# Order of the relu sums in the last token group, and of a product and a transpose early on

## The chip, the cores and the metric

The kernel runs on one core of a Trainium2 chip. The metric is device time in microseconds (us). Its time before the change is 225.6 us, the median of three runs (225.09, 225.60 and 230.58).

## What is computed

Attention with a window ("LM-infinite"), then a mixer. There are 4 batches (B), 8 heads (H) of width 64 (D) and 768 positions (S). Each query sees 8 global keys and the 96 keys up to itself:

```python
scores = scale * np.matmul(q, k.transpose(0, 1, 3, 2))
...
keep = is_global | is_local
...
scores = scores + bias          # -slope of the head * distance
scores = np.where(keep, scores, -1000000000.0)
a = np.exp(scores - max); a = a / sum(a)
attn = np.matmul(a, v)
```

The heads are put side by side to x of 768 x 512 per batch, and then

```python
h = xt @ U @ V                  # low rank, 32, over the positions
u = x + h.transpose(0, 2, 1)
ch = np.maximum(u @ w_ch1, 0.0) @ w_ch2      # 512 -> 2048 -> 512
return u + ch
```

Inputs and output are 32-bit floats; the kernel casts to 16 bits for its matmuls.

## The kernel before, in words

**Engines and order.** The program's order is written by hand: one `manual_schedule` covers it all, and each engine runs its own instructions in the order in which the code issues them. PE does matmuls and transposes, DVE and ACT the work between them and PE's accumulation banks, POOL casts, SP starts most loads and all stores. An instruction waits on the engine of its operands' producers, and on those who still use the buffer that it writes. Behind a waiting instruction its whole engine waits. PE's weight loads (PEld) run ahead of its matmuls.

**Pairs of heads.** The unit of the attention is a pair of heads: 4 pairs (NP) per batch, 16 in all, numbered through, so pairs 0 to 3 are batch 0 and pair 4 is the first of batch 1. In the main loop of batch 0 (L965 to L1011, one turn per pair i) these stages are issued:

- `st_T(i)` (L247): PE transposes q and k of a pair (twelve matmuls, L259). ACT copies qT (L281), DVE copies kT (L282) and a small part of kA (L287), the keys as the neighbouring block needs them, with the global ones in front.
- `st_KA(i)` (L292): DVE copies the rest of kA from kT (L295).
- `st_A(i)`, `st_P(i)` (L320): vA, the values as kA needs them. POOL copies it, and st_P has DVE put the 8 global rows in (L322).
- `st_SE(i, c)` (L381), a third c of the scores: matmuls with the bias on PE (L364, L372, L379), the exponential on ACT (L391, L396).
- `st_V(i, hi)` (L440), v's product for one head: eleven matmuls into a bank "ob" (L449, L453), DVE takes the reciprocals of the sums (L458), and DVE multiplies into x_sb (L472). In the last pair of batch 0 (pair 3) ACT multiplies head 0 straight into the 16-bit x (six instructions, L467), and DVE head 1 (L464); both write x16 of the same pair, in different columns. For head 1 of pairs 0 to 2, ACT copies x into the 16-bit x16 later (L1009, `last_x`).
- `st_M1(i)` (L478) multiplies x16 with U on PE (L492), DVE copies the result (L496). `st_M2(i)` (L504) multiplies with V and adds x (L509, L514); the result uT is copied by DVE (L520) or ACT (L522).
- `st_R()` (L400): DVE halves the bias table once (L402, "the table's half"), in turn 3.

For pair 3 (i = 3) the turn issues, in this order: scores, third 0; cast_v, st_A; st_V(2, 0); load_v(4); st_M1(1); scores, third 1; st_T(4); st_V(2, 1); st_KA(4); st_P(3); st_R; scores, third 2; the ACT copy L1009; st_M2(1). Behind the loop (L1012 on) follow st_V(3, 0), the first scores of pair 4, st_M1(2), st_V(3, 1), a cast on POOL (L124), st_M2(2), the first matmuls of the up-projection (L557), st_M1(3) and st_M2(3). From L1027 on comes the steady loop, in which the attention of later pairs is interleaved with the mixer's matmuls.

**The mixer.** The tokens of a batch form 3 groups of 256 (FT). Up-projection and relu give htr (16 blocks of 128 channels, L822 and L827; in batch 3 through seven products on sums, `queue_products`, L695 on PE, with L670 on DVE and L704, L745 on ACT). The down-projection of batches 1 to 3 goes by Winograd's variant of Strassen (`queue_group`, L781): htr is cut into a11, a12, a21, a22 (channel half by token half), and DVE forms

```
s1 = a21 + a22    s2 = s1 - a11    s3 = a11 - a21    s4 = a12 - s2
```

(`queue_sums`, L791, instruction L576; s3 overwrites a21). Each product (`mk_product`, L880) is eight matmuls on PE (L890) into one half of a bank, cx or cy, and then an add of that half into x_sb on DVE (L895). The products are x1 (a11), y1 (a12), x2 (s2), y2 (s1), x3 (s3), y3 (s4) and x4 (a22). In the last group of all (batch 3, group 2) they are issued x1, y2, x2, y1, x3, y3, and then `end_product` (L866), which takes the seventh in two halves of 128 columns (L872, L877) with a store behind each (L836).

A sum isn't issued to DVE when it is queued. `queue_sum` (L573) puts it into a list (`jobs` for the s, `slow` for the t, the sums of weights); `fill` (L930) takes it out when it is due, between two products. `need` (L580) takes sums out ahead of a product until the named ones are there. `queue_sums(k)` is called twice for each group: k = 0 when the first half of the channels' blocks is there, k = 1 with the second. s1 and s2 are made in two halves, one in each call. s3 and s4 are made whole in the second call, but in the last group in two halves too (128 x 512 each, in place of 128 x 1024). In the last group the second call comes right behind the last product of the up-projection (row (2, 1, 4): group 2, channel set 1, product 4), which is issued behind x1 and ahead of y2.

Of the kernel before, what the change touches and what calls it, by code (L numbers as in the profile page):

```python
# [20 lines left out]
def kernel(  # L21
# [24 lines left out]
    NP = H // 2  # L46
# [41 lines left out]
    def ps_cps(name, dtype=FP32, cols=512):  # L88
        return psum.tile([P, cols], dtype, name=name, tag="cps", bufs=2)

    def ps_th(name, dtype=FP32, cols=512):
        return psum.tile([P, cols], dtype, name=name, tag="th", bufs=3)
# [74 lines left out]
    def warm(n, cols=512):  # L167
        wps = ps_cps("warm")
        for _ in range(n):
            nc.tensor.matmul(wps[:, 0:cols], zw[:, 0:P], zw[:, 0:cols], start=True, stop=True)  # L170
# [76 lines left out]
    def st_T(i):  # L247
        stq, stk = cast.pop(i)
        qT = kp.tile([P, S], FP16, name="qT", tag="qT")
        kT = kp.tile([P, S], FP16, name="kT", tag="kT")  # L250
        kA = kp.tile([P, NSB - 1, P], FP16, name="kA", tag="kA")
        tps = []
        for st in (stq, stk):
            if i == 0 and st is stk:
                warm(4, P)
            tp = ps_th("tp", FP16, S) if i < NP + 2 else ps_cps("tp", FP16, S)
            tps.append(tp.rearrange("d (n p) -> d p n", n=NSB))
            for n in range(NSB):
                nc.tensor.matmul(  # L259
                    tp[:, n * P:(n + 1) * P], st[:, n].rearrange("s h d -> s (h d)"), ident16,  # L260
                    is_transpose=True, start=(n == 0), stop=(n == NSB - 1),
                )
        tq, tk = tps
        qts[i] = qT
        if i == 0:
            kts[i], kas[i] = kT, kA
            for a in range(2):
                ts, ps = slice(a * GT, (a + 1) * GT), slice(a * P // 2, (a + 1) * P // 2)
                nc.scalar.copy(qT[:, ts].rearrange("d (p n) -> d p n", n=NSB), tq[:, ps])
                nc.vector.tensor_copy(kT[:, ts].rearrange("d (p n) -> d p n", n=NSB), tk[:, ps])  # L270
                ns = slice(0, 2) if a == 0 else slice(2, NSB - 1)
                nc.vector.tensor_copy(
                    kA[:, ns].rearrange("d n p -> d (n p)"), kT[:, ns.start * P:ns.stop * P]
                )
                ns = slice(max(1, ns.start), ns.stop)
                nc.vector.tensor_copy(
                    kA[:, ns, 0:NG],
                    kT[:, 0:NG].unsqueeze(1).broadcast_to((P, ns.stop - ns.start, NG)),
                )
            return  # L280
        nc.scalar.copy(qT.rearrange("d (p n) -> d p n", n=NSB), tq)  # L281
        nc.vector.tensor_copy(kT.rearrange("d (p n) -> d p n", n=NSB), tk)  # L282
        kts[i], kas[i] = kT, kA
        if i > NP:
            st_KA(i, nc.gpsimd)
        else:
            nc.vector.tensor_copy(  # L287
                kA[:, :, 0:GC].rearrange("d b (p n) -> d b p n", n=NSB),
                tk[:, 0:GC // NSB].unsqueeze(1).broadcast_to((P, NSB - 1, GC // NSB, NSB)),
            )  # L290

    def st_KA(i, eng):  # L292
        kT, kA = kts[i], kas[i]
        if i <= NP:
            eng.tensor_copy(  # L295
                kA[:, :, GC:], kT.rearrange("d (n p) -> d n p", n=NSB)[:, 0:NSB - 1, GC:]
            )
            return
        eng.tensor_copy(kA.rearrange("d n p -> d (n p)"), kT[:, 0:S - P])
        eng.tensor_copy(  # L300
            kA[:, 1:, 0:NG], kT[:, 0:NG].unsqueeze(1).broadcast_to((P, NSB - 2, NG))
        )
# [17 lines left out]
    def st_P(i):  # L320
        eng = nc.gpsimd if i == NPE - 1 else nc.vector
        eng.tensor_copy(  # L322
            vas[i][0:NG, 1:].rearrange("p n h d -> p n (h d)"),
            vts[i][0:NG, 0:1].rearrange("p n h d -> p n (h d)").broadcast_to(
                (NG, NSB - 2, 2 * (D + 1))
            ),
        )
# [72 lines left out]
    def st_R():  # L400

        nc.vector.tensor_scalar_mul(relcat2[:, 1], relcat, 0.5)  # L402
# [170 lines left out]
    def queue_sum(name, part, out_, a, b_, op, wait=0):  # L573

        def go():
            nc.vector.tensor_tensor(out_, a, b_, op)  # L576
            have.add((name, part))
        (slow if name[0] == "t" else jobs).append((count[0] + wait, go, name))

    def need(*names):  # L580

        for queue, kind in ((jobs, tuple), (slow, str)):
            while not all(n in have for n in names if isinstance(n[0], kind)):
                queue.popleft()[1]()
# [19 lines left out]
    def weight(w, j):  # L604
        return tw[w][:, j] if w != "t3" else tw[w][j // 2][:, j % 2]
# [175 lines left out]
    def queue_group(b, g):  # L781
# [7 lines left out]
        last = (b, g) == (B - 1, NFG - 1)  # L789

        def queue_sums(k):  # L791

            h = cell["htr"]
            if k == 0:
                for x in (1, 2, 4):
                    cell[f"s{x}"] = ffp.tile([P, HJ, P], FP16, name=f"s{x}", tag=f"s{x}", bufs=1)
                cell.update(a11=h[:, 0:HJ, 0:P], a12=h[:, HJ:NJC, 0:P],
                            a21=h[:, 0:HJ, P:FT], s3=h[:, 0:HJ, P:FT], a22=h[:, HJ:NJC, P:FT])
            for name, a, b_, op in (
                ("s1", "a21", "a22", ALU.add), ("s2", "s1", "a11", ALU.subtract),  # L800
                ("s3", "a11", "a21", ALU.subtract), ("s4", "a12", "s2", ALU.subtract),
            ):
                parts = {k: slice(k * HJ // 2, (k + 1) * HJ // 2)}
                if name in ("s3", "s4") and not last:
                    parts = {0: slice(0, HJ)} if k else {}
                for part, js in parts.items():
                    queue_sum(
                        (name, b, g), part, cell[name][:, js], cell[a][:, js], cell[b_][:, js],
                        op, wait=0 if last else 2 - k,
                    )  # L810
# [69 lines left out]
        def mk_product(bank, half, a, w, dst, first=False, done=None, more=()):  # L880

            def go():
                if bank not in cell:
                    cell[bank] = ps_cps(bank)
                need(*(((a, b, g), k) for k in range(2 if last or a in ("s1", "s2") else 1)
                       if a[0] == "s"))
                need(*((w, k) for k in range(4 if w == "t3" else 2) if w[0] == "t"))
                ps = cell[bank][:, half]
                for j in range(HJ):
                    nc.tensor.matmul(  # L890
                        ps, cell[a][:, j], weight(w, j), start=(first and j == 0),
                        stop=(done is not None and j == HJ - 1), skip_group_check=True,
                    )
                for n, cs in (dst, *more):
                    nc.vector.tensor_tensor(x_sb[:, n, cs], ps, x_sb[:, n, cs], ALU.add)  # L895
                for what in done or ():
                    store(*what)
            return go
# [66 lines left out]
    for i in range(NP):  # L965
        st_SE(i, 0)
        cast_v(i)
        st_A(i)
        if i:
            st_V(i - 1, 0)  # L970
        if i == 0:
            load_uv()
        if i < 2:
            load_v(i + 2)
        if i == 1:
            load_qk(NP)
        if i == 2:
            load_qk(NP + 1, nc.gpsimd)
        if i == 3:
            load_v(NP)  # L980
        if i == NP - 1:
            st_M1(i - 2)
        if 0 < i < NP - 1:
            st_T(i + 1)
        st_SE(i, 1)
        if i == NP - 1:
            st_T(i + 1)
        if i == 2:
            st_M1(i - 2)
        if i:  # L990
            last_x = st_V(i - 1, 1)
        else:
            st_T(i + 1)
        st_KA(i + 1, nc.vector)
        st_P(i)
        if i == 0:
            cast_qk(i + 2, nc.vector)
        elif i < 3:
            cast_qk(i + 2, nc.gpsimd)
        if i == 1:  # L1000
            nc.gpsimd.tensor_copy(u16[:, :, 0:R], ust)
            load_w1(0)
        if i == 2:
            load_w1(1)
        if i == NP - 1:
            st_R()
        st_SE(i, 2)
        if i:
            nc.scalar.copy(*last_x)  # L1009
        if i >= 2:  # L1010
            st_M2(i - 2)  # L1011
# [15 lines left out]
    for i in range(NP, NPAIR + 2):  # L1027
        b, hp = divmod(i, NP)
# [140 lines left out]
```

## Time and profile before

| what | value |
|---|---|
| runs, all (us) | 225.09, 225.60, 230.58 |
| their median (us) | 225.60 |
| the profiled execution, its own time (us) | 224.96 |
| its span, first to last instruction (us) | 223.2 |
| PE's granted clock over the span | 1.00 |

The span is 1.76 us shorter than the execution's own time. Times in rows of the trace count from the span's start. In a row of the timeline stand the start, the length, the engine, the line, the operation and its tiles with sizes, and in brackets how long the engine was idle ahead of it and who ended that wait. In the chain of waits, which is followed back from the last instruction, "issue" is time in which the engine waited for nothing that the profile shows. Instructions of one engine overlap in the rows where the next one's start lies ahead of the last one's end.

### The profile page before, as it was taken

What the parts mean: (1) busy time and instruction counts of PE and PEld (TensorE: products, weight loads), DVE (VectorE), ACT (ScalarE), POOL (GpSimd) and SP (SyncE); (2) the same over time, 40 slices, a digit from 0 to 9 for tenths busy, and PEclk for the clock granted to TensorE, in tenths of its full rate; (3) what the DMA queues carried; (4) which work ended last, traced back from release to release, by engine and by line L of the source; (5) the groups of instructions that cost most, each with busy time, mean ns of one, the idle gap of its engine ahead of it and who ended that gap; (6) DMA issues with size and microseconds to landing.
All of it is one profiled execution on the core that took longest, in us unless ns stands there. A gap on an engine that the chain in (4) does not pass through costs nothing.

```text
span 223.2 us, 6285 instructions
## 1 busy us (share of the span) xinstructions
PE 216.3 (97%) x2577; PEld 172.5 (77%) x2579; DVE 174.8 (78%) x360; ACT 135.7 (61%) x215; POOL 74.0 (33%) x124
## 2 busy tenths in 40 slices
PE   7989999999999999999999999999999999999994
PEld 3556678788754546888888888888989999999973
DVE  3698775749488988598979698979798588878774
ACT  6787967785806253968594847382833556556620
POOL 6499638297547422322222222323112000000000
PEclk9999999999999999999999999999999999999999
DMA  6999999979998989898999995855240601102022
GB/s 200 327 290 245 261 229 260 319 142 173 195 171 177 200 212 258 207 255 190 212 249 205 241 222 118 156 147 38 80 82 17 117 0 50 50 3 94 3 94 95
DMA packets 86709, 36.75 MB, mean 165 GB/s; under 512 B 74169, under 2 KB 83737, under 8 KB 86681
## 3 DMA queue, kind: packets, MB, share of 16 engines
q1 hardware_dynamic: 82408, 32.11, 62.5%
q0 software_dynamic: 4272, 4.24, 12.4%
q8 instruction: 20, 0.33, 0.6%
q14 instruction: 9, 0.07, 0.1%
HBM read 27.46 MB, written 6.29 MB: 151 GB/s over the span
## 4 chain that ended last, share of the span: by engine, by line
PE 90%; DVE 7%; ACT 2%; issue 1%
PE hps L822 27%; PE cx L890 13%; PE cy L890 10%; PE cps L857 10%; PE hps L695 6%; PE sc L372 4%; PE tp L259 3%; PE ob L453 3%; PE ob L449 2%; PE sc L538 2%; PE warm L170 2%; PE sc L379 2%; PE ob L695 1%; PE sc L695 1%; PE sc L364 1%; DVE x_sb L895 1%
## 5 line engine op out<-in xcount | busy, mean ns | idle before, releaser
L822 PE MATMUL hps<-uT,w 128*128 128x256 f16 x564 | 70.6, 273 | 0.0
L827 ACT ACTIVATE htr<-hps 128x512 f16<-128x512 f32 x72 | 42.2, 601 | 33.4 <-PE hps L822 33.3
L822 PEld LDWEIGHTS <-w 128*128 128x128 f16 x564 | 52.4, 98 | 6.8
L418 DVE SCALAR_TENSOR_TENSOR sp<-sc,relcat 128x1024 f32<-128x1024 f32 (+1 forms) x27 | 32.1, 1188 | 8.3 <-PE sc L379 4.1
L436 ACT ACTIVATE ep<-sp 128x1408 f16<-128x1408 f32 x24 | 33.2, 1384 | 0.0
L475 POOL CAST x<-x_sb 128x384 f16<-128x384 f32 x27 | 14.2, 526 | 48.5 <-DVE x_sb L472 45.3
L890 PEld LDWEIGHTS <-htr 128*128 128x128 f16 x280 | 25.9, 98 | 2.8
L857 PE MATMUL cps<-w,htr 128*128 128x512 f16 x96 | 23.9, 379 | 0.0
L890 PEld LDWEIGHTS <-s 128*128 128x128 f16 x216 | 19.8, 98 | 3.4 <-DVE s L576 1.0
L546 POOL CAST x<-x_sb 128x768 f16<-128x768 f32 x12 | 10.6, 884 | 33.3 <-DVE x_sb L543 29.9
L895 DVE TENSOR_TENSOR x_sb<-cx,x_sb 128x256 f32<-128x256 f32 x36 | 15.0, 418 | 8.3 <-PE cx L890 7.9
L372 PEld LDWEIGHTS <-kT 64*128 64x128 f16 x192 | 8.7, 93 | 11.5 <-issue 10.1
L472 DVE TENSOR_TENSOR x_sb<-ob,rcp 128x384 f32<-128x384 f32 x30 | 16.7, 557 | 1.1
L745 ACT ACTIVATE htr<-htr 128x512 f16<-128x512 f16 x18 | 11.3, 630 | 9.3 <-DVE htr L670 9.3
L453 PE MATMUL ob<-v,ep 128*128 128x65 f16 x192 | 16.3, 194 | 0.3 <-DVE x_sb L472 0.3
L372 PE MATMUL sc<-qT,kT 64*128 64x128 f16 x192 | 15.7, 220 | 0.3
L453 PEld LDWEIGHTS <-ep 128*128 128x128 f16 x192 | 13.7, 98 | 2.7 <-issue 0.5
L895 DVE TENSOR_TENSOR x_sb<-cy,x_sb 128x256 f32<-128x256 f32 x27 | 11.3, 420 | 5.3 <-PE cy L890 4.9
L857 PEld LDWEIGHTS <-htr 128*128 128x128 f16 x96 | 8.4, 97 | 8.3
L449 PE MATMUL ob<-vA,ep 128*128 128x65 f16 x160 | 14.3, 194 | 0.3 <-DVE vA L322 0.2
L143 POOL CAST v<-vst 128x768 f16<-128x768 f32 x16 | 13.5, 842 | 3.2 <-DMA vst<-in_v_dram 3.2
L543 DVE TENSOR_TENSOR x_sb<-sc,x_sb 128x768 f32<-128x768 f32 x12 | 11.5, 958 | 3.7 <-PE sc L538 3.6
(141 smaller groups left out, 419.2 us busy)
## 6 DMA issues: line engine op xcount, KB each, us to landing
qst<-in_q_dram SPq DMA_DIRECT2D x16, 384.0 KB, 3.8
kst<-in_k_dram SPq DMA_DIRECT2D x16, 384.0 KB, 6.3
vst<-in_v_dram SPq DMA_DIRECT2D x16, 384.0 KB, 4.7
out_dram<-x_sb SPq DMA_DIRECT2D x23, 256.0 KB, 2.1
w<-in_moe_w_ch_dram POOLq DMA_DIRECT2D x8, 512.0 KB, 8.6
vA<-v SPq DMA_DIRECT2D x8, 152.3 KB, 3.4
uT<-x SPq DMA_TRANSPOSE x12, 4.5
kT<-k SPq DMA_TRANSPOSE x8, 3.2
```

What stands on the lines that cost most here:

```text
L372: nc.tensor.matmul(scs[hi][:, o:o + P], kT[r, kb * P:(kb + 1) * P], qT[r, kb * P:(kb + 1) * P], start=(o == 0 and not on_pe), stop=(o + P ...
L418: nc.vector.scalar_tensor_tensor(out=sps[i][:, :, c0:c0 + tot], in0=both[:, :, 0:tot], scalar=qk_scale / slope[2 * (i % NP)], in1=relfs[c0 ...
L436: nc.scalar.activation(eps[i][:, hi], sps[i][:, hi], AF.Exp, scale=slope[2 * (i % NP)])
L449: nc.tensor.matmul(ob[:, qi], ep[:, OF[qi - 1]:OF[qi - 1] + P], vA[:, qi - 1, hi], start=True, stop=False,)
L453: nc.tensor.matmul(ob[:, qi], ep[:, DG[qi]:DG[qi] + P], vt[:, qi, hi], start=(qi == 0), stop=True,)
L472: nc.vector.tensor_tensor(xo, ob[:, :, 0:D], rb, ALU.mult)
L695: nc.tensor.matmul(ps[:, j * P:(j + 1) * P], uw[st][a][:, dc, j * P:(j + 1) * P], turns[g][t][:, dc], start=(k in (1, 2, 5) and j == 0 and ...
L822: nc.tensor.matmul(hps[:, k * FT:(k + 1) * FT], w1_16[:, dc, jt * P:(jt + 1) * P], uT[:, dc, ts], start=(dc == 0 and k == 0), stop=(dc == ...
L827: nc.scalar.activation(cell["htr"][:, 2 * jp:2 * jp + 2].rearrange("p j t -> p (j t)"), hps, AF.Relu)
L857: nc.tensor.matmul(cps, htr[:, jc, t * P:(t + 1) * P], w2_16[:, jc], start=(b > 0 and jc == 0), stop=(jc == NJC - 1),)
L890: nc.tensor.matmul(ps, cell[a][:, j], weight(w, j), start=(first and j == 0), stop=(done is not None and j == HJ - 1), skip_group_check=True,)
L895: nc.vector.tensor_tensor(x_sb[:, n, cs], ps, x_sb[:, n, cs], ALU.add)
```

## The change

There are two parts, with no instruction added to PE and no DMA touched.

Part 1, the last group of the mixer. s3 and s4 are formed whole, in the second call of `queue_sums`, as in the other groups; so two instructions replace four. `mk_product` no longer asks for two halves of s3 and s4 there. Ahead of y2 (the product with s1) it asks for the second half of s2, and then for both halves of s1; as the jobs stand in one list, s1's second half, then s2's second half are issued ahead of y2. s3 is then issued when it is due or when x3 asks for it, s4 likewise with y3, behind s1 and s2.

Part 2, turn i = 3 of the loop of batch 0. `st_V(2, 1)` is issued ahead of `st_T(4)`, where it came behind it; `st_P(3)` is issued ahead of `st_KA(4)`, where it came behind it. The other turns issue what they did, in the same order.

```diff
@@ queue_sums
                 parts = {k: slice(k * HJ // 2, (k + 1) * HJ // 2)}
-                if name in ("s3", "s4") and not last:
+                if name in ("s3", "s4"):
                     parts = {0: slice(0, HJ)} if k else {}
@@ mk_product
                     cell[bank] = ps_cps(bank)
-                need(*(((a, b, g), k) for k in range(2 if last or a in ("s1", "s2") else 1)
+                if last and a == "s1":
+                    need((("s2", b, g), 1))
+                need(*(((a, b, g), k) for k in range(2 if a in ("s1", "s2") else 1)
                        if a[0] == "s"))
@@ main loop of batch 0
         st_SE(i, 1)
-        if i == NP - 1:
-            st_T(i + 1)
         if i == 2:
             st_M1(i - 2)
         if i:
             last_x = st_V(i - 1, 1)
-        else:
+        if i == 0 or i == NP - 1:
             st_T(i + 1)
+        if i == NP - 1:
+            st_P(i)
         st_KA(i + 1, nc.vector)
-        st_P(i)
+        if i < NP - 1:
+            st_P(i)
```

## The prediction

> **What bounds the kernel now.** The head of the page comes first, then the busy time by stretches, then the chain that ended last.
>
> ```profile
> span 223.2 us, 6285 instructions
> PE 216.3 (97%) x2577; PEld 172.5 (77%) x2579; DVE 174.8 (78%) x360; ACT 135.7 (61%) x215; POOL 74.0 (33%) x124
> ```
>
> The stretches' columns are busy time and count for PE, PEld, DVE, ACT and POOL, then the granted clock, the DMA share and GB/s.
>
> ```profile
> 0.00:33.00 33.00, 29.91 (x376) 19.05 (x379) 23.62 (x62) 24.93 (x44) 22.28 (x44) 1.00 1.04 259
> 33.00:211.00 178.00, 177.82 (x2114) 146.18 (x2113) 143.92 (x280) 108.58 (x169) 51.68 (x80) 1.00 0.74 152
> 211.00:223.20 12.20, 8.61 (x92) 7.27 (x89) 7.23 (x20) 2.22 (x4) 0.00 (x0) 1.00 0.25 88
> ```
>
> Between 33 and 211 us PE is busy 177.82 of 178.00: nothing but less PE work shortens that stretch. PE has holes only before 33 us and after 211 us, and each half of the change lies in one of them. A hole closed ahead of 33 us moves everything behind it forward, as long as PE goes on from its own queue. The change alters no matmul count, no store and no load, so its whole worth is holes closed or opened.
>
> **Part 1, the last group.** The chain of waits over the last group's products (start, length, what):
>
> ```profile
> 214.00 0.44 PE cy L890 x4
> 214.44 0.04 issue
> 214.48 0.62 PE cy L890 x4
> 215.10 0.02 issue
> 215.13 0.42 DVE x_sb L895
> 215.55 0.34 DVE s L576
> 215.89 0.05 issue
> 215.94 0.61 PE cx L890 x4
> 216.55 0.55 PE cy L890 x5
> ```
>
> From the start of y2 (214.00) to the start of y1 (216.55) lie 2.55 us for sixteen matmuls. Four of them unstalled take 0.44, sixteen 1.75: 0.80 us is lost. The second hole is the larger: x2's second half needs the second half of s2, which stands on DVE's queue behind y2's add, and that add cannot run before y2 is through. On DVE (timeline of that engine):
>
> ```profile
> 205.88 0.68 DVE L576 TENSOR_TENSOR s<-htr,s 128x1024 f16<-128x1024 f16 x1
> 206.48 0.42 DVE L895 TENSOR_TENSOR x_sb<-cx,x_sb 128x256 f32<-128x256 f32 x1
> ...
> 213.68 0.41 DVE L895 TENSOR_TENSOR x_sb<-cx,x_sb 128x256 f32<-128x256 f32 x1
> 214.01 0.41 DVE L576 TENSOR_TENSOR s<-htr 128x512 f16<-128x512 f16 x1
> ```
>
> The 213.68 row is x1's add, the 214.01 row the second half of s1. Work that DVE has ready starts 0.33 apart at half size (213.68 to 214.01) and 0.60 apart for a whole sum (205.88 to 206.48). What the change does here, step by step:
>
> - Removed ahead of x1's add: the first halves of s3 and s4. x1's eight matmuls end at about 213.57 (y2 starts 0.44 behind them: between lies the up-projection's last product, eight matmuls of L695), so the add can start at 213.60, not 213.68. Half s1 follows at 213.93, ends 0.41 later at 214.34, and PE resumes y2 at 214.40 instead of 214.48: 0.08 gained. The wait before it stays, 0.13 of 0.21.
> - Half s2 is issued ahead of y2 by the added need. It reads s1, so it starts when s1 is written, at about 214.38, and ends at 214.79. PE asks for it 0.87 behind 214.40, at 215.27. The second hole (0.80 less 0.21, 0.59) closes. What is queued behind this on DVE is y2's add, whose product ends near 215.05: it isn't delayed.
> - Added behind y2's add: s3 whole (0.60 of queue), x2's add (0.33), s4 whole (0.60), y1's add. From 215.05: s3 from 215.39 to 216.07, x2's add 215.99, s4 216.33 to 217.01, y1's add 216.93 to 217.36. PE without stall starts x3 (needs s3 and x2's add, through at 216.41) at 216.59, and y3 (needs s4 and y1's add) at 217.46. Both are met, y3 with 0.10 to spare. If that cover goes, y3 waits; with 0.86 in place of 0.68 for the whole sums it would wait some 0.26.
>
> Sum of part 1: 0.08 + 0.59 = 0.67 us gained; bounds 0.40 (y3 waits 0.26) and 0.80 (every hole closed). The last product, its adds and the store are moved as they are.
>
> **Part 2, the last pair of batch 0.** The chain (first fence) and DVE's timeline (second):
>
> ```profile
> 26.04 0.51 ACT x L1009
> 26.56 0.65 ACT uT L522 x2
> 27.21 0.05 issue
> 27.25 1.35 ACT x L467 x6
> 28.60 0.17 issue
> 28.77 0.57 DVE x L464
> ```
>
> ```profile
> 20.50 0.75 DVE L295 COPY kA<-kT 128x580 f16<-128x580 f16 x1
> ...
> 24.23 0.96 DVE L282 COPY kT<-tp 128x768 f16<-128x768 f16 x1 [0.89 <-PE tp L259]
> 25.11 0.21 DVE L287 COPY kA<-tp 128x60 f16<-128x60 f16 x1
> 25.23 0.18 DVE L458 RECIPROCAL rcp<-ob 128x6 f32<-128x6 f32 x1
> 25.45 0.56 DVE L472 TENSOR_TENSOR x_sb<-ob,rcp 128x384 f32<-128x384 f32 x1
> 25.93 0.33 DVE L295 COPY kA<-kT 128x580 f16<-128x580 f16 x1
> 26.17 0.27 DVE L322 COPY vA<-v 8x520 f16<-8x520 f16 x1
> 26.37 0.54 DVE L402 TENSOR_SCALAR relcat<-relcat 128x768 f32<-128x768 f32 x1
> ...
> 28.05 0.20 DVE L458 RECIPROCAL rcp<-ob 128x6 f32<-128x6 f32 x1
> ```
>
> - v's product of pair 2, head 1 goes in front of pair 4's twelve transposes on PE. Eleven matmuls swap places with twelve transposes: PE's sum is unchanged. The product takes 0.34 (its rows stand 0.03 apart), so the transposes end 0.34 later, and DVE's idle 0.89 before 24.23 is where the product's reciprocal and multiply now go. They start near 23.89 and end at 24.68 (0.22 between them, then 0.56), 1.33 sooner than 26.01. kT's copy follows at 24.60, kA's small part 25.47, the vA rows (st_P) 25.60 to 25.87, kA's rest 25.79 to 26.12, the table's half 26.04 to 26.58. kA is 0.14 sooner, the vA rows 0.57.
> - PE has drained its queue at 25.74 and today waits for the multiply, then for the vA rows (its next products run at 26.16 and 26.50). Now it starts pair 3's first product at 25.74, waits 0.09 for the vA rows, and everything behind runs 0.58 sooner: scores of pair 4, M1(2), v's second product, its reciprocal at 27.46 instead of 28.05.
> - ACT's rows:
>
> ```profile
> 23.46 1.02 ACT L391 ACTIVATE ep<-sc 128x1024 f16<-128x1024 f32 x1 [0.40 <-PE sc L379]
> 24.38 0.79 ACT L281 COPY qT<-tp 128x768 f16<-128x768 f16 x1
> ```
>
> qT's copy waits for ACT's own exponential, not for the transposes: q's six are through near 24.20 even 0.34 later. So ACT gains only what L1009 no longer waits for the multiply (26.01): at most 0.09.
>
> The crux is L464, the multiply that PE's next stall waits for:
>
> ```profile
> 29.38 0.34 PEld L492 LDWEIGHTS <-u 128*128 128x128 f16 x6 [0.33 <-DVE x L464]
> ```
>
> It starts 0.52 behind its reciprocal's end (28.25); L472 starts 0.04 behind its own (25.41, 25.45). Either it truly follows ACT's six L467, as the chain has it, and then part 2 is worth L1009's 0.09; or it is held for a fixed time, and then it moves with the reciprocal, by 0.58. The code speaks for the second: L464 reads the other head's bank and its own rcp and writes the other columns, and its start is 0.17 behind ACT's end where a true release costs 0.02 to 0.05 in the chain above. If it isn't held at all any more, M1(3) starts when PE is through, at 28.58: 0.80. Bounds of part 2: 0 and 0.80; I take 0.58.
>
> A rule that speaks against part 2, row first: kA's copy took 0.75 at 20.50 with POOL's cast beside it, 0.33 at 25.93 without. The next cast is here:
>
> ```profile
> 26.32 1.28 POOL L124 CAST q<-qst 128x768 f16<-128x768 f32 x1 [1.40 <-DMA qst<-in_q_dram]
> ```
>
> [...]
>
> No instruction moves on POOL's or SP's queue, and no DMA. Downstream, later loads may not come sooner; behind 33 us I see none that PE waits for.
>
> **Sum.** The profiled execution took 224.96: 224.96 - 0.67 - 0.58 = 223.71. The median of the runs, 225.60, holds one of 230.58; the undisturbed ones are 225.09 and 225.60, 0.13 and 0.64 above the profiled one. A median of such runs lies some 0.2 above, so I forecast 223.9.
>
> **The rivals.**
>
> - L464 does follow ACT. For it: the chain and the bracket of that row. Against: the code, and the lag of 0.17. PE then idles 0.7 before M1(3). 224.96 - 0.67 - 0.09 = 224.2, as a median 224.4.
> - It hardly does what it says: at the end DVE is slower than its rows (y3 waits), and early the gain is absorbed by a landing that stays. 224.96 - 0.40 - 0.0 = 224.56, as a median 224.8. Against: the 0.10 and 0.33 computed margins.
> - Slower: kA's copy meets POOL's cast. Place: DVE at 25.79 to 26.12. Point: the cast begins ahead of kA's copy, by data 0.5 sooner or a copy 0.5 later. Price, with the longest cast shown: kA ready at 26.32 + 1.28 + 0.19 = 27.79 (0.19 is what the copy at 20.50 ended behind its cast), scores of pair 4 1.58 later than I have them, part 2 a loss of 1.0: 224.96 - 0.67 + 1.0 = 225.3. Against: today's copies at the same times escape it.
>
> **How the numbers follow.** My forecast, with L464 held or free, 0.58 (223.4 to 224.3 with the runs' spread); L464 behind ACT 0.24; hardly anything 0.12; slower 0.06. The range 223.2 to 225.0 reaches from L464 free (224.96 - 0.67 - 0.80 = 223.49, less 0.3 of spread) over the first two rivals to 0.2 above the second, and leaves out some 0.15. Two per cent, about what a measurement of this kernel can tell from no change, is 4.5 us, and no case reaches it: within 0.96; faster 0.02 and slower 0.02 are left for disturbed runs.
>
> **What would show it.** Right: the hole before x2's second half gone and x1's add straight ahead of both half sums; PE from y2 to y1 1.88 instead of 2.55; y3 without a wait; L472 of pair 2 near 24.1; pair 3's first product near 25.74; M1(3) near 28.8. L464 tells the cases apart: 0.5 behind its reciprocal near 28.2 (mine), 0.04 behind it (free), or 0.17 behind the last L467 near 28.7 (the rival). Wrong would make me a stall of PE in front of y3, kA's copy over 0.5, or a new PE hole behind 33 us.

## The result and the profile after

| what | before | after |
|---|---|---|
| median of 22 runs each (us) | 226.14 | 224.68 |
| ratio, 95% interval | | 0.9943 [0.9921, 0.9964] |
| profiled execution, its own time (us) | 224.96 | 224.69 |
| its span (us) | 223.2 | 222.9 |

The ratios here and below leave out executions that were disturbed (more than 1.5% above the kernel's fastest). The median is 0.8 above the forecast of 223.9 and within its range of 223.2 to 225.0; the ratio means 1.3 us of gain, where the sum had 1.25. Measured twice more, on other chips, the same kernel gave 1.0024 [0.9985, 1.0062] and 0.9961 [0.9923, 0.9999]. Weighted by their intervals (inverse squares of the widths) the three make 0.996, some 0.85 us. The first two intervals don't overlap, so something besides the change differs between these measurements, and 0.996 is a rough middle. A change of half a per cent is small against the spread of single executions (223.45 to 227.45 after the change), so the rows of the trace have to carry the argument.

The busy time by stretches, after, for the middle of the span (columns as in the prediction):

```profile
33.00:211.00 178.00, 177.44 (x2110) 145.83 (x2108) 143.81 (x279) 108.36 (x168) 52.05 (x80) 1.00 0.73 151
```

PE lacks 0.56 of the 178.00 in the middle, where it lacked 0.18. The one new hole is in PE's timeline at 133 us (the last row here; the others are used further on):

```profile
26.41 0.19 PE L453 MATMUL ob<-v,ep 128*128 128x65 f16 x1
26.68 0.19 PE L449 MATMUL ob<-vA,ep 128*128 128x65 f16 x1
...
29.34 0.50 PE L492 MATMUL tmp_ps<-x,u 128*128 128x128 f16 x6
...
133.21 0.70 PE L822 MATMUL hps<-uT,w 128*128 128x256 f16 x5 [0.47 <-DMA uT<-x]
```

**The last group.** The chain, and DVE's timeline, after (the added lines move L890 to L892 and L895 to L897):

```profile
214.38 1.02 PE cy L892 x8
215.40 0.87 PE cx L892 x8
216.27 0.87 PE cy L892 x8
217.14 0.87 PE cx L892 x8
218.02 0.87 PE cy L892 x8
```

```profile
213.97 0.42 DVE L897 TENSOR_TENSOR x_sb<-cx,x_sb 128x256 f32<-128x256 f32 x1 [0.45 <-PE cx L892]
214.31 0.42 DVE L576 TENSOR_TENSOR s<-htr 128x512 f16<-128x512 f16 x1
214.76 0.42 DVE L576 TENSOR_TENSOR s<-s,htr 128x512 f16<-128x512 f16 x1
215.43 0.42 DVE L897 TENSOR_TENSOR x_sb<-cy,x_sb 128x256 f32<-128x256 f32 x1 [0.25 <-PE cy L892]
215.78 0.68 DVE L576 TENSOR_TENSOR htr<-htr 128x1024 f16<-128x1024 f16 x1
216.37 0.42 DVE L897 TENSOR_TENSOR x_sb<-cx,x_sb 128x256 f32<-128x256 f32 x1
216.71 0.68 DVE L576 TENSOR_TENSOR s<-htr,s 128x1024 f16<-128x1024 f16 x1
217.31 0.42 DVE L897 TENSOR_TENSOR x_sb<-cy,x_sb 128x256 f32<-128x256 f32 x1
```

DVE is no longer the step between y2 and x2: x2 is one piece of 0.87. y2's start to y1's takes 1.89 instead of 2.55, and x3 and y3 follow without a wait. y2 itself takes 1.02: the first hole is still there, as forecast.

**The early part.** DVE's and ACT's timelines, after:

```profile
26.21 0.42 DVE L322 COPY vA<-v 8x520 f16<-8x520 f16 x1
26.55 0.32 DVE L295 COPY kA<-kT 128x580 f16<-128x580 f16 x1
...
28.23 0.20 DVE L458 RECIPROCAL rcp<-ob 128x6 f32<-128x6 f32 x1
28.52 0.56 DVE L464 TENSOR_TENSOR x<-ob,rcp 128x384 f16<-128x384 f32 x1
```

```profile
24.06 1.02 ACT L391 ACTIVATE ep<-sc 128x1024 f16<-128x1024 f32 x1 [0.40 <-PE sc L379]
...
27.68 1.37 ACT L467 ACTIVATE x<-ob,rcp 128x64 f16<-128x64 f32 x6
```

This execution was 0.60 late before the changed order began: the exponential of pair 3's second third starts at 24.06, before at 23.46. That is the zero from here on. M1(3) then starts 5.28 behind it (29.34), before 5.92 (29.38 less 23.46). The two profiled executions add up: 224.96 + 0.60 (late start) - 0.64 (early part) - 0.66 (last group) + 0.47 (hole at 133 us) = 224.73, and 224.69 was measured.

### The profile page after: what moved, and what is told of

It is laid out like the page before. It is cut to its first block, busy times and chain, and to the rows that moved or that the text cites. A ratio compares the mean times of both kernels' runs of the same rounds, so it can differ in the third digit from the quotient of the medians.

```text
span 222.9 us, 6282 instructions
## 1 busy us (share of the span) xinstructions
PE 215.8 (97%) x2577; PEld 171.9 (77%) x2579; DVE 175.2 (79%) x358; ACT 135.6 (61%) x215; POOL 74.3 (33%) x124
## 3 DMA queue, kind: packets, MB, share of 16 engines
HBM read 27.46 MB, written 6.29 MB: 151 GB/s over the span
## 4 chain that ended last, share of the span: by engine, by line
PE 88%; DMA 5%; DVE 2%; ACT 1%; SPq 1%; POOL 1%; issue 1%; DVEq 0%
PE hps L822 28%; PE cx L892 13%; PE cy L892 10%; PE cps L857 10%; PE hps L695 6%; PE sc L372 4%; DMA vst<-in_v_dram 3%; PE ob L453 3%; PE sc L538 2%; PE tp L259 2%; PE ob L449 2%; DMA uT<-x 2%; PE sc L379 2%; PE ob L695 1%; PE sc L695 1%; PE sc L364 1%
## 5 line engine op out<-in xcount | busy, mean ns | idle before, releaser
L892 PEld LDWEIGHTS <-htr 128*128 128x128 f16 x280 | 26.0, 98 | 2.7
L892 PEld LDWEIGHTS <-s 128*128 128x128 f16 x216 | 19.9, 98 | 2.7 <-DVE s L576 0.2
L897 DVE TENSOR_TENSOR x_sb<-cx,x_sb 128x256 f32<-128x256 f32 x36 | 15.0, 419 | 8.8 <-PE cx L892 8.6
L897 DVE TENSOR_TENSOR x_sb<-cy,x_sb 128x256 f32<-128x256 f32 x27 | 11.3, 420 | 4.7 <-PE cy L892 4.4
```

What stands on the lines that cost most here:

```text
L892: nc.tensor.matmul(ps, cell[a][:, j], weight(w, j), start=(first and j == 0), stop=(done is not None and j == HJ - 1), skip_group_check=True,)
```

## The experiments

Three yardsticks are read from each profile: from the exponential to M1(3); from L464's reciprocal's end to L464; from y2's start to y1's, and to the start of the very last add (6.10 before, 214.00 to 220.10; 5.44 after, 214.38 to 219.82).

**Each part alone.** `part1_alone` is the changed kernel with the old main loop, `part2_alone` the old kernel with the new main loop.

> The last group's part of the change alone. If the two parts add (my theory), y2's start to y1's start takes 1.88 instead of 2.55, y3 waits for nothing, and the ratio to the kernel before is 0.997 (0.67 of 225.6 gained). The early stage is that of before: from the exponential of pair 3's second third of the scores to M1(3) 5.92, with L464 0.5 behind its reciprocal if that pause belongs to the kernel, 0.1 if it was an accident of one execution. Rival, the early part's gain is taken back later by transfers and all of the gain is here: ratio 0.994.

> The early part alone. If the parts add: the exponential to M1(3) in 5.3 instead of 5.92, y2 to y1 2.55 as before, ratio 0.9975 (0.58 gained). Rival, what is gained early is given back where PE waits for a landing of uT (0.47 in the changed kernel's profile, none in the profile before): the early stage is shorter but the ratio is 1.000, and PE waits for uT again behind 33 us.

Measured: 0.9977 [0.994, 1.0014] and 0.9978 [0.9939, 1.0016]. Each interval holds 1, so the times alone say little; their sizes (0.5 us each) are roughly those of two halves that add. The rows are sharper. Part 1 alone has y2 to y1 in 1.89 (214.86 to 216.75), 5.44 to the last add, and the early stage of before, 5.91. Part 2 alone has 2.55 and 6.10, and 5.13 early. DVE and PE in part 2 alone, then DVE in part 1 alone:

```profile
27.41 0.20 DVE L458 RECIPROCAL rcp<-ob 128x6 f32<-128x6 f32 x1
27.71 0.56 DVE L464 TENSOR_TENSOR x<-ob,rcp 128x384 f16<-128x384 f32 x1
```

```profile
28.53 0.50 PE L492 MATMUL tmp_ps<-x,u 128*128 128x128 f16 x6
```

```profile
28.64 0.20 DVE L458 RECIPROCAL rcp<-ob 128x6 f32<-128x6 f32 x1
29.36 0.56 DVE L464 TENSOR_TENSOR x<-ob,rcp 128x384 f16<-128x384 f32 x1 [0.52 <-ACT x L467]
```

The pause ahead of L464 (0.52 in both kernels with the old loop, 0.10 with the new one) belongs to the kernel. Part 1 alone, whose early stage is the old one, also waits 0.45 for uT behind 33 us, and part 2 alone doesn't: the hole comes without the early gain, so it isn't that gain given back.

**The two halves of part 1.** `no_need` takes the added need out of the changed kernel; `halves_need` keeps it and restores the halves.

```diff
-                if last and a == "s1":
-                    need((("s2", b, g), 1))
```

```diff
-                if name in ("s3", "s4"):
+                if name in ("s3", "s4") and not last:
...
-                need(*(((a, b, g), k) for k in range(2 if a in ("s1", "s2") else 1)
+                need(*(((a, b, g), k) for k in range(2 if last or a in ("s1", "s2") else 1)
```

> The changed kernel without the added need: whole s3 and s4, but y2 asks only for s1. My theory: s2's second half comes behind y2's add again, the second hole of 0.59 is back, y2 to y1 takes 2.47. Rival, the shorter queue of DVE is all that matters, and the planner issues s2's second half in time: 1.88.

> The changed kernel with s3 and s4 in halves again, but with the added need. My theory: the second hole stays closed, the first is 0.21 instead of 0.13 as the first halves of s3 and s4 delay x1's add and s1: y2 to y1 1.96. Rival, whole sums close the hole: 2.47. The early stage is that of the changed kernel and tells whether L464's 0.09 behind its reciprocal comes again.

The chain of `no_need`, then of `halves_need`:

```profile
216.06 1.03 PE cy L890 x8
...
217.12 0.42 DVE x_sb L895
217.54 0.34 DVE s L576
217.89 0.05 issue
217.93 0.62 PE cx L890 x4
...
218.58 0.42 DVE x_sb L895
219.00 0.61 DVE htr L576
...
219.66 1.05 PE cx L890 x8
```

```profile
214.20 0.44 PE cy L892 x4
...
215.29 0.87 PE cx L892 x8
216.17 0.87 PE cy L892 x8
```

Without the need the second hole is back (y2 to y1 2.50; 2.47 expected), and, which I had not expected, whole sums then do harm: x2's add comes late, s3 stands behind it, and x3 waits for s3. From y2 to the last add it takes 6.51 (216.06 to 222.57), 0.41 more than before the change. With the need and halves it takes 5.52 (214.20 to 219.72), y2 to y1 1.97 (1.96 expected). So the need brings 0.58, whole sums 0.08 on top, and whole sums alone lose 0.41. Each of these figures compares single profiled executions.

**What holds L464.** DVE's order in the programs offers a clue: the new order saves DVE one waiting instruction (ahead of the reciprocal, L458), so L464 is the 64th of DVE's program and not the 65th. This count is of the program, with its waiting instructions; among the working rows of DVE's timeline L464 is the 58th in both. `after_shift1` (first diff) adds one instruction to the changed kernel, `before_shift4` (second) four to the old one.

```diff
-    nc.vector.memset(zw, 0.0)
+    nc.vector.memset(zw, 0.0); nc.vector.memset(zw, 0.0)
```

```diff
-    nc.vector.memset(zw, 0.0)
+    for _ in range(5): nc.vector.memset(zw, 0.0)
```

> The changed kernel with one more DVE instruction at the very start (the zeroing of a tile, done twice), so that L464 is again the 65th instruction of DVE's program, as it was before the change; in the changed kernel it is the 64th. Theory P (place): the pause of 0.5 ahead of L464 belongs to the 65th place of DVE's program and comes back: L464 0.5 behind its reciprocal, and from the exponential of pair 3's second third to M1(3) 5.35 instead of 5.13. Theory A (L464 follows ACT's six L467): it stays at 0.10, and 5.13.

> The kernel before with four more DVE instructions at the very start (the same zeroing, repeated), nothing else; L464 goes from the 65th to the 69th place of DVE's program. Theory P: the pause is gone, L464 0.10 behind its reciprocal, the exponential to M1(3) 5.50 instead of 5.92. Theory A: L464 0.17 behind the last L467 as before, 0.52 behind its reciprocal, and 5.92.

DVE in `after_shift1`, then DVE, ACT and POOL in `before_shift4`:

```profile
26.31 0.56 DVE L322 COPY vA<-v 8x520 f16<-8x520 f16 x1 [0.38 <-POOL vA L308]
...
28.48 0.20 DVE L458 RECIPROCAL rcp<-ob 128x6 f32<-128x6 f32 x1
29.19 0.56 DVE L464 TENSOR_TENSOR x<-ob,rcp 128x384 f16<-128x384 f32 x1 [0.52 <-ACT x L467]
```

```profile
26.91 0.69 DVE L295 COPY kA<-kT 128x580 f16<-128x580 f16 x1
...
29.39 0.20 DVE L458 RECIPROCAL rcp<-ob 128x6 f32<-128x6 f32 x1
29.69 0.56 DVE L464 TENSOR_TENSOR x<-ob,rcp 128x384 f16<-128x384 f32 x1
```

```profile
28.60 1.34 ACT L467 ACTIVATE x<-ob,rcp 128x64 f16<-128x64 f32 x6 [0.30 <-DVE rcp L458]
```

```profile
26.58 0.83 POOL L124 CAST q<-qst 128x768 f16<-128x768 f32 x1
```

One instruction more at the start of the changed kernel, and the pause is back (0.51); four more in the old one, and it is gone (0.10), with L464 starting at 29.69 while ACT's six run to 29.94. Theory A has fallen: the pause belongs to the 65th place in DVE's program. In the first profile after, too, L464 starts (28.52) while ACT's six run (to 29.05). The program says why: L464's wait on ACT is met by an earlier copy of line L1009, done at 16.60 in the profile before, and not by L467; the bracket there names an engine that merely ended its work shortly before. Only the places 64, 65 and 69 were seen. The totals missed (6.10 and 6.07 from the exponential to M1(3); 5.35 and 5.50 expected), for a reason of their own: in the first the vA rows waited for POOL's vA, in the second kA's copy ran into POOL's cast and took 0.69.

**The order of the two copies and of the product.**

`p_first` has the transposes ahead of the product again, `ka_first` kA's copy ahead of the vA rows, each against the changed kernel:

```diff
         st_SE(i, 1)
+        if i == NP - 1:
+            st_T(i + 1)
...
             last_x = st_V(i - 1, 1)
-        if i == 0 or i == NP - 1:
+        else:
             st_T(i + 1)
```

```diff
-        if i == NP - 1:
-            st_P(i)
         st_KA(i + 1, nc.vector)
-        if i < NP - 1:
-            st_P(i)
+        st_P(i)
```

> The changed kernel with pair 4's transposes ahead of v's product again, but with st_P(3) ahead of st_KA(4). L464 is at the 65th place. Pair 3's first product waits for the vA rows 0.25 less, and what is behind it comes 0.25 sooner; ACT's L467 don't move. Theory P: L464 0.5 behind its reciprocal, the exponential to M1(3) 5.67. Theory A: L464 stays 0.17 behind the last L467, 5.92.

> The changed kernel with v's product ahead of the transposes, but st_KA(4) ahead of st_P(3) as before the change. The vA rows come 0.24 later, pair 3's first product waits for them that much longer: the exponential to M1(3) 5.37 instead of 5.13. Rival, the order of the two copies is without effect: 5.13.

Neither settles its question: 6.29 in both. DVE in `p_first`, then in `ka_first`:

```profile
26.51 0.90 DVE L322 COPY vA<-v 8x520 f16<-8x520 f16 x1
...
29.02 0.20 DVE L458 RECIPROCAL rcp<-ob 128x6 f32<-128x6 f32 x1
29.73 0.56 DVE L464 TENSOR_TENSOR x<-ob,rcp 128x384 f16<-128x384 f32 x1 [0.52 <-ACT x L467]
```

```profile
26.24 0.67 DVE L295 COPY kA<-kT 128x580 f16<-128x580 f16 x1
26.83 0.84 DVE L322 COPY vA<-v 8x520 f16<-8x520 f16 x1
```

The vA rows took 0.84 (`ka_first`) and 0.90 (`p_first`) beside POOL's casts, 0.27 without. `p_first` has L464 at the 65th place, and 0.51 behind its reciprocal. What the order of the two copies is worth stays open.

**The hole at 133 us.** `store_behind` holds the stores of batches 1 and 2 that SP would issue ahead of uT's transfer until that one is issued.

```diff
-            if b:
-                go()
+            if b:
+                after_x.append(go) if hold[0] else go()
...
+        hold[0] = NP + 1 < i <= NPAIR
...
         if i > NP + 1:
             st_X(i - 1)
+        hold[0] = False
+        while after_x:
+            after_x.popleft()()
```

> The changed kernel with three stores of batches 1 and 2 moved behind the transposing transfer of uT that they stood in front of on SP's queue (no other work moved). In four of ten profiles, of kernels with and without the early part of the change, PE waits 0.34 to 1.05 for the last quarter of batch 2's uT near 133 us, and the transfer is issued 0.28 to 1.64 behind the end of the cast that it reads, with a store just ahead of it. Theory S (SP's queue sets this landing): the transfer is issued within 0.3 of the cast's end, PE has no wait for uT there, and the time is that of the changed kernel or up to 0.5 less: ratio 0.992 to 0.995. Rival, the transfer itself is slow whenever other transfers share the engines: the wait is there in spite of the earlier issue, same ratio as the changed kernel.

> The changed kernel again, beside the other of this call. The parts sum: ratio 0.9945 (0.67 for the last group, 0.79 less the wait for the vA rows for the early part, of 226). L464 0.10 behind its reciprocal, y2 to y1 1.89; if the copies of DVE meet POOL's casts, the wait for the vA rows is 0.4 to 1.1, which is no part of the change.

Measured: 0.9952 [0.992, 0.9984] for `store_behind`, and 1.0024 [0.9985, 1.0062] for the changed kernel beside it, which misses the 0.9945 expected. SP and POOL in `store_behind`:

```profile
126.52 1.24 SPq L527 DMA_TRANSPOSE uT<-x  x1
```

```profile
125.66 0.83 POOL L546 CAST x<-x_sb 128x768 f16<-128x768 f32 x1 [2.90 <-DVE x_sb L543]
```

The transfer is issued 0.03 behind the cast's end (126.49), and PE has no hole there. Two profiles with the stores moved show none (this and `w1_behind`); of twelve without, five do. That fits theory S, without proof that a single execution was helped. The two ratios lie 0.0072 apart, or 1.6 us, where theory S allows 0.5; the cause of the rest stays open. The second profile of the changed kernel has L464 0.10 behind its reciprocal and y2 to y1 1.88, but M1(3) at 5.98. POOL, DVE and PE there:

```profile
24.87 0.73 POOL L308 COPY vA<-v 128x650 f16<-128x650 f16 x1
```

```profile
25.63 0.56 DVE L322 COPY vA<-v 8x520 f16<-8x520 f16 x1 [0.48 <-POOL vA L308]
```

```profile
28.91 0.50 PE L492 MATMUL tmp_ps<-x,u 128*128 128x128 f16 x6
```

Its exponential starts at 22.93, so POOL's copy of vA ends 2.67 behind it. PE wants it at 2.3 now (26.35 less 24.06 in the first profile); the old order wanted it at 2.70. POOL was late because pair 4's k, which POOL casts ahead of v, had landed late. Of eight profiles with the changed early stage, four had vA late; in two of these PE also waited 1.0 and 1.4 for k's cast itself, which the old order needs no later. No profile of the old order has k as late, so what that order would lose there isn't shown.

**The chain on POOL shortened.** `w1_behind` is `store_behind` with one more move:

```diff
         cast_v(i)
         st_A(i)
+        if i == NP - 1:
+            load_w1(1)
...
-        if i == 2:
-            load_w1(1)
```

> The kernel with the three stores moved behind uT's transfer, and on POOL's queue the issue of the second w1 load (0.74 us of POOL) moved from ahead of pair 3's cast of v to behind its copy of vA. Theory V: under the changed order pair 3's first product needs the vA rows at 2.3 behind the exponential of the second third; where pair 4's k lands late, POOL's chain (cast of k, issue of the load, cast of v, copy of vA) ends at 2.57 to 2.67 and the early part's gain is lost (M1(3) at 5.98 in the changed kernel's second profile instead of 5.13). With the issue out of that chain vA is ready 0.74 sooner, M1(3) at 5.13 to 5.3, and the ratio is below that of the changed kernel beside it: about 0.993. Rival, the landing is so rarely late that nothing is seen: the ratio of the kernel with the stores moved alone, 0.995; or the load of w1 now lands too late (needed near 37, estimated landing near 34) and PE waits for w.

> The changed kernel a third time, beside the other of this call, since its ratio was 0.9943 [0.9921, 0.9964] first and 1.0024 [0.9985, 1.0062] on another chip. If the parts are worth 0.67 and 0 to 0.79 according to when pair 4's k lands: 0.994 to 0.999. If the second measurement is right and the first a chance: 1.000 or more.

Measured: 0.989 [0.9838, 0.9941] for `w1_behind`, 0.9961 [0.9923, 0.9999] for the changed kernel. The first rests on three executions of six (223.03, 223.12, 223.34), and the intervals overlap: it is the best version by its number, on thin ground. Its profile has M1(3) at 5.13 and no wait for w, but k landed early there, so theory V was not put to the test. `after_third` had k late: PE waited 1.0 for its cast, 0.4 for POOL's vA, 0.4 for the rows, and 0.5 for uT.

## Why the prediction was right, and where it was not

- **Part 1, right in each step.** 0.67 was forecast, 0.66 measured. The profile after is 0.38 later where y2 starts (214.38 for 214.00); with that taken off, x1's add is at 213.59 (213.60 forecast), the halves of s1 and s2 at 213.93 and 214.38 (213.93, 214.38), s3 215.40 (215.39), x2's add 215.99 (215.99), s4 216.33 (216.33), y1's add 216.93 (216.93), and y3 comes without a wait. `no_need` and `halves_need` show the mechanism, the order of s2 ahead of y2's add.
- **Part 2, the total right, two terms wrong.** 0.58 was forecast; 0.64 in the first profile, 0.79 in the four whose vA and copies met nothing (`part2_alone`, `halves_need`, `store_behind`, `w1_behind`). That 0.58 came so near 0.64 is luck: the pause's end brought 0.21 more, and the vA rows cost 0.15 more. The failed step is "or it is held for a fixed time, and then it moves with the reciprocal": the pause neither followed ACT nor moved along. It hung on the 65th place of DVE's program, and the change took a waiting instruction out ahead of it (place 65 to 64). Counting instructions, not only their durations, would have shown it as possible. The forecast's own bound for that case, PE through at 28.58, is what part 2 alone measured (28.53, its exponential 0.06 earlier).
- **"waits 0.09 for the vA rows"** was 0.24 in the first profile: the rows' copy took 0.42, not 0.27, beside POOL's cast of x (25.97 to 26.48, in the fence below). The product was moved towards data whose slack on POOL I hadn't worked out; vA was named only for its rows on DVE. Late k takes the early part's gain away: M1(3) at 5.98 instead of 5.13.
- **L464 behind ACT** (the first rival, 0.24) is refuted by `before_shift4`. A cast of POOL doesn't hold L464 either, by the first profile after: there L464 (28.52) runs beside POOL's cast of k (28.22 to 29.05), 0.10 behind its reciprocal and at its usual 0.56. **"It hardly does what it says"** has its early half come true in executions with k late (a landing that stays takes the gain); y3 never waited.
- **The baseline, "some 0.2 above"**, was too small: the kernel before had a median of 226.14 when measured beside the change, 1.18 above the profiled execution. That is why 223.9 was 0.8 low while the gain of that measurement was right.
- **The slower rival**, kA's copy meeting POOL's cast, had one row for it: the copy at 20.50 began 0.26 behind a cast of POOL (20.24, 0.82 long) and ended 0.19 behind its end, 0.75 in all. In the runs it was seen where kA's copy goes ahead of the vA rows: it took 0.69 in `before_shift4`, which has the old order, and 0.67 in `ka_first`. In the ten profiles with the vA rows first kA took 0.32, and it is the rows that met casts (0.42 to 0.90 in six of them). In the first profile after, the cast of q (26.43) began ahead of kA's copy (26.55), and still the copy took 0.32:

```profile
25.97 0.51 POOL L475 CAST x<-x_sb 128x384 f16<-128x384 f32 x1
26.43 1.60 POOL L124 CAST q<-qst 128x768 f16<-128x768 f32 x1
```

The vA rows were running at 26.43, and it was the cast that stretched, to 1.60; at 27.27 in `part2_alone`, with no copy of DVE beside it, the cast of q took 0.83. So the rival's "point" was put too simply. The same is seen in `after_again` and `after_third`, where the cast of q also began while the vA rows ran: it took 1.46 and 1.60, and kA's copy 0.32. But in `ka_first` it began while kA's copy ran (26.66) and took 0.88. What decides which of two such instructions is slowed, these rows don't show.
- **"A new PE hole behind 33 us"** was to make me wrong, and one of 0.47 came. The early part isn't needed for it: part 1 alone has it (0.45) with the old early stage, and part 1 acts only near 214 us. Neither profile of the unchanged work (the kernel before, `before_shift4`) has it, so that the change makes it no likelier isn't shown.

## What to carry to other kernels

A sum made whole is cheaper only if nothing urgent stands behind it: here the order (s2 ahead of y2) was worth 0.58, the size 0.08, and the size without the order cost 0.41. A product moved forward is worth what its latest operand allows, so the slack of each operand counts, also of those made on a quiet engine. And a pause that no semaphore explains is tested by shifting the program by an instruction, before a mechanism is made up for it.

## What the runs showed of the hardware

In the four kernels that had L464 at the 65th place of DVE's program (the one before, `part1_alone`, `after_shift1`, `p_first`) it started 0.51 to 0.52 behind its reciprocal's end, in the other ten 0.09 to 0.11; the place cost some 0.42. In the profiles before and after, no other instruction of DVE started more than 0.12 behind the last of what it waited for and the instruction ahead of it. In the changed kernel the 65th is L520, which starts 0.48 behind L464's start, as in `before_shift4`, where it has another place: in 0.48 a pause of 0.42 has room beside the instruction ahead of it (an estimate from the two figures). What the pause is, no run shows.
